# A weight stream in 12 whole units through four places, in place of 21 halves through seven

## The chip, the core and the metric

The kernel runs on one core of a Trainium2 chip. Its engines are TensorE (PE, with weight loads PEld), VectorE (DVE), ScalarE (ACT), GpSimd (POOL) and SyncE (SP), which here only issues DMAs; SP, ACT and POOL each have a DMA queue, and all queues share 16 DMA engines. SBUF has 128 partitions, and a tile "of 4 KB" holds 4 KB in each. The metric is the device time of one execution in microseconds (us), lower is better; several runs are taken and their median is compared.

## What is computed

Two attention blocks over the same 2048 x 640 input are mixed by a gate. Block A walks through 64 segments of 32 rows one after the other: the 8 memory rows that a segment puts out are the first 8 rows of the next segment's input, so the segments can't overlap freely.

```
x = A_x
g = sigmoid((x * gate_w).sum(-1, keepdims=True))
a = A(x, mem0, Wq, Wk, Wv, Wo)     # 32 heads of 192, Dm = 640
b = B(x, wqkv, wo)                 # sliding, dilated local attention
return g * a + (1 - g) * b

# A, for each of 64 segments:
h = concatenate([mem, xs], axis=1)            # 8 + 32 rows
q, k, v = h @ Wq, h @ Wk, h @ Wv              # 640 x 6144 each
p = softmax(mask(q @ k^T * scale))
o = (p @ v) @ Wo                              # 6144 x 640
mem = o[:, :8]; outs.append(o[:, 8:])
```

## The kernel before

**Order of the whole.** Block B runs first (`part_b`), then a prepass for A (`prepass`), which computes q, k and v of the segments' last rows for all segments at once, then the loop over segments (`part_a`), then the output projection of the rows that the prepass covers (`part_z`). The loop body is `segment("rest", ...)` of one segment followed by `segment("head", ...)` of the next.

**Weights.** The weights of A are cut into slices of 128 partitions, named by matrix and place. (q, p, kc) and (k, p, kc), with p = 0 to 2 and kc = 0 to 4, and (v, t, kc) have 4 KB a partition; (oa, i), i = 0 to 11, and (ob, i), i = 0 to 7, are the output weights with 3 KB a partition. A slice can be cut into two halves (a name with one more number, `_is_half`, `_parts`). Each segment reads every slice once, in the order of the code: q(0,0), k(0,0), q(1,0), q(0,1), q(0,2), k(0,1), k(0,2), q and k (0,3) and (0,4), the rest of q(1,*), k(1,*), q(2,*), k(2,*), then v(0,*), v(1,*), v(2,*), then oa and ob. A q, k or v slice is read by one burst of four matmuls of 512 columns, one for each group of 32 PE columns (`m_qk` L818, `m_v` L916); an output slice by `o_group` (L980). Between them stand the small matmuls of attention: `scores` (L870), `e_sum` (L894), `pv_half` (L941, L947), and `pick` (L997), which makes the next segment's memory rows.

**Resident and streamed.** Not all weights fit in SBUF. Most slices are loaded once and stay (`res_tiles`: wres early, wlate later). Those in `STREAM` are loaded anew in each segment, in the order of `STREAM`, into a ring of places (`slots`, tiles wst): unit n goes to place n modulo `SLOTS`. Before the change these are 21 halves (15 of 2 KB, 6 of 1.5 KB) and seven places of 2 KB. `pump` issues on SP's queue every next unit whose place is free; `release`, called behind the matmuls that read a slice, frees its place and pumps (L562 is the issue). Because SP runs in order, unit n + 1 is not issued ahead of unit n.

**Stages of the loop.** The loop body is split into four stages (`stage`, L1133 for the loop's own waits). `held()` makes SP wait, at that point of its program, for the DMAs that it issued one stage earlier, and holds back further units until the next `stage()`. No engine enters a stage before all have finished the stage two before it. The boundaries are: before `scores(1)`; behind oa 0 to 3; in the head behind q(1,0); and the loop's end. The program order of SP in one iteration is so: units freed by q(2,*), k(2,*) and the first v slices; held; units freed by later v slices; the load of the next segment's aP from zpk_dram (L752); held; units freed by oa and ob; held; in the head, units freed by the last ob and by q(0,*), k(0,*), k(1,*).

**Other transfers in a segment.** POOL's queue loads aVz (96 KB, L756), aK from in_xh_dram and from selx_dram, and stores oz_dram twice (48 KB each, L759); ACT's queue loads aG and stores out_dram (30 KB each).

**Other uses of the places.** In part B and the prepass the same tiles serve as staging for columns of Wq and Wk (`get_columns`, L599) and of v (`v_columns`, `get_slice`, L585) that are not resident. One end of place 1 also holds `st4`, the copy of a q product between ACT (L829) and DVE (L837).

**The end.** In the last segment SP issues the loads of oz (`load_oz`, L1155, four tiles at a time into resident slices no longer needed), ACT and DVE sort them (`sort_oz`), and `part_z` multiplies them (L1192), adds to a tile `b4` of B's rows (L1196) and stores. The `b4` tiles are resident half slices.

Of the kernel before, what the change touches and what calls it, by code (L numbers as in the profile page):

```python
# [11 lines left out]
F32 = mybir.dt.float32  # L12
I32 = mybir.dt.int32

SLOTS = 7
N_EARLY = 15
N_EARLY2 = 12
N_LAST = 7
LATE0 = 71680
STREAM = [("q", 0, 1, 1), ("k", 0, 1, 1), ("k", 0, 3, 1), ("q", 1, 1, 0), ("k", 1, 0, 0), ("k", 1, 3, 1), ("q", 2, 2,  # L20
          0), ("k", 2, 0, 1), ("k", 2, 1, 1), ("k", 2, 4, 1), ("v", 0, 3, 1), ("v", 1, 1, 0), ("v", 1, 4, 1), ("v", 2,
          0, 1), ("v", 2, 3, 0), ("oa", 3, 1), ("oa", 4, 1), ("ob", 2, 0), ("oa", 7, 0), ("oa", 11, 0), ("ob", 6, 0)]

STEP_PE = 3.4

# [7 lines left out]
def _width(key):  # L33
    n = 1536 if key[0] in ("oa", "ob") else 2048
    return n // 2 if _is_half(key) else n

def _parts(key):
    halves = [key + (h,) for h in range(2)]
    return halves if any(k in STREAM for k in halves) else [key]

# [53 lines left out]
class _K:  # L94
# [398 lines left out]
    def v_columns(self, t, kc):  # L493

        out = []
        for k in _parts(("v", t, kc)):
            sl = self.get_slice(k)
            out += [sl[:, f:f + 512] for f in range(0, _width(k), 512)]
        return out
# [11 lines left out]
    def weights_setup(self):  # L511
        nc, tc = self.nc, self.tc
        rest = [k for u in _slice_keys() for k in _parts(u) if k not in STREAM]
        first = ["q", "k", "v", "oa", "ob"]
        rest = sorted(rest, key=lambda k: first.index(k[0]))
        self.early, self.early2, late = rest[:N_EARLY], rest[N_EARLY:N_EARLY + N_EARLY2], rest[N_EARLY + N_EARLY2:]
        self.late = ([], [], late[-N_LAST:])
        used = 0
        for k in late[:-N_LAST]:
            used += 2 * _width(k)  # L520
            self.late[int(used > LATE0)].append(k)
        self.wres = self.ctx.enter_context(tc.tile_pool(name="wres", bufs=1))
        self.res_tiles = {}
        at = _places()[0]
        self.packed = {k: self.laid["slices"][n:n + 128 * _width(k)].rearrange("(p f) -> p f", p=128) for k, n in at.items()}
        self.wscr = self.packed
        self.wstream = self.ctx.enter_context(tc.tile_pool(name="wstream", bufs=1))
        self.slots = [self.wstream.tile([128, 1024], BF, name=f"wst{i}") for i in range(SLOTS)]
        self.slot_at, self.streaming, self.pending = 0, False, []

    def load(self, key, t):
# [42 lines left out]
    def get_slice(self, key):  # L574
        if key in self.res_tiles:
            return self.res_tiles[key]
        n = _width(key)
        if self.streaming:
            assert STREAM[self.used] == key and self.used < self.sent
            t = self.slots[self.used % SLOTS][:, 0:n]  # L580
            self.used += 1
            return self.view(t, key)
        t = self.slots[self.slot_at % SLOTS][:, 0:n]
        self.slot_at += 1
        self.nc.gpsimd.dma_start(t, self.wscr[key])  # L585
        return self.view(t, key)

    def get_columns(self, m, h):

        W = {"q": self.Wq, "k": self.Wk}[m].rearrange("(c p) f -> p c f", p=128)  # L590
        p, x = h // 2, h % 2
        out = {}
        for kc in range(self.KC):
            if (m, p, kc) in self.res_tiles:
                t = self.res_tiles[m, p, kc][:, 1024 * x:1024 * x + 1024]
            else:
                t = self.slots[self.slot_at % SLOTS]
                self.slot_at += 1
                (self.nc.sync if m == "q" else self.nc.gpsimd).dma_start(t[:], W[:, kc, 1024 * h:1024 * h + 1024])  # L599
            out[kc] = [t[:, f:f + 128] for f in range(0, 1024, 128)]  # L600
        return out

# [97 lines left out]
    def part_a(self):  # L700
# [4 lines left out]
        with ctx:  # L705
# [28 lines left out]
                        return x[:, f:f + 32]  # L734

            st = [Px[2], Px[1], KW[:, 512:1024], Px[2]]
            st4 = self.slots[1][:, 768:1024], Px[0][:, 0:256]
            st5 = (P[1][:, 1:5, 0:8, :].rearrange("p b c i -> p b (c i)"), Px[0][:, 256:512])

            psm = ctx.enter_context(tc.tile_pool(name="psm", bufs=1, space=bass.MemoryType.PSUM))  # L740
# [44 lines left out]
            def segment(part, prev, s, nxt, looped=False):  # L785
# [278 lines left out]
                if nxt is None:  # L1064
                    self.oz, self.oz_keys = {}, {}
                    self.oz_free = [k for p in range(3) for m in "qk" for k in self.res_tiles if k[:2] == (m, p) and len(k) == 3]
                    self.oz_free += [k for k in self.res_tiles if k[0] == "v" and len(k) == 3]
                    self.b4_free = [k for k in self.res_tiles if k[0] in "vqk" and len(k) == 4]
                    self.load_oz(0)
                if nxt is not None:  # L1070
                    load_seg(nxt)
# [97 lines left out]
    def part_z(self, psm, wo, tail):  # L1169

        nc = self.nc
        oz = self.oz
        kept = self.kept.values()
        for i, k in enumerate(k for k in STREAM if k in wo and k not in kept):
            t = self.res_tiles[self.b4_free[4 + i]][:, 0:_width(k)]
            nc.sync.dma_start(t, self.wscr[k])
            wo[k] = self.view(t, k)
        for n in range(1, 4):
            if n > 1:
                self.load_oz(n)  # L1180
            self.sort_oz(n)
        for n in range(4):
            b4 = self.res_tiles[self.b4_free[n]][:, 0:640]
            rows = lambda ap: ap.rearrange("(n s t) f -> n s t f", n=4, t=32)[n, :, 24:32, :]
            nc.scalar.dma_start(b4.bitcast(I32).rearrange("p (j f) -> p j f", j=4),
                                self.bsc_dram.rearrange("(n s t) j f -> n s t j f", n=4, t=32)[n, :, 24:32, :, 0:80])
            for part, f0, nf in (("oa", 0, 384), ("ob", 384, 256)):
                ps = psm[int(part == "ob")]
                for c in range(48):
                    R, j, t = c // 12, c // 3 % 4, c % 3  # L1190
                    for q in range(4):
                        nc.tensor.matmul(ps[32 * q:32 * q + 32, 0:nf],  # L1192
                                         lhsT=oz[n, q][:, 24 * (1 - R // 2) + 6 * j + 3 * (R % 2) + t, :],
                                         rhs=self.o_weights(wo, part, c), start=(c == 0), stop=(c == 47),
                                         tile_position=(0, 32 * q), skip_group_check=True)
                nc.vector.scalar_tensor_tensor(out=b4[:, f0:f0 + nf], in0=ps[:, 0:nf], scalar=self.gZ[:, n:n + 1],  # L1196
                                               in1=b4[:, f0:f0 + nf], op0=ALU.mult, op1=ALU.add)
            nc.sync.dma_start(rows(self.out2d), b4)
            if n == 0:
                tail()  # L1200
# [63 lines left out]
```

## Time and profile before

| | us |
|---|---|
| Median of 3 runs | 1554.49 (1550.25 to 1554.56) |
| The profiled execution: its own time | 1550.84 |
| its span | 1548.8 |

| Stretch, us from the start | What runs | PE busy | DMA share | GB/s |
|---|---|---|---|---|
| 0 to 180 | part B | 145.9 of 180 | 0.76 | 205 |
| 180 to 294 | prepass q, k | 112.0 of 114 | 0.81 | 235 |
| 294 to 344 | prepass v | 49.5 of 50 | 0.84 | 236 |
| 344 to 400 | first segments | 43.4 of 56 | 0.89 | 290 |
| 400 to 1400 | the loop | 195 to 197 of each 200 | 0.96 to 0.97 | 321 to 326 |
| 1484 to 1502 | loads of oz, sorting | 11.7 of 18 | 0.82 | 188 |
| 1502 to 1548 | output projection | 42.1 of 46 | 0.12 | 29 |

The DMA share is the mean share of time in which the 16 DMA engines had a packet in hand; the granted TensorE clock is 1.00 in all of the loop's stretches. An engine's busy time is the union of its instructions, so PE counts as busy also where only one of four column groups works. In names such as `wst<-in_slices_dram` the target stands left; "SPq" is SP's instruction queue, which issues DMAs and waits.

### The profile page before, as it was taken

The numbers are of one execution on the slowest core, as the hardware profiler recorded it, in microseconds if no ns is written. First come the engines' busy times: TensorE is split into PE (matmuls) and PEld (weight loads), VectorE is DVE, ScalarE is ACT, GpSimd is POOL, SyncE is SP. The second block draws the span as 40 slices with busy tenths as digits, with TensorE's granted clock in tenths as the row PEclk, the third lists the DMA queues.
The fourth block names the chain that finished last, engine by engine and source line by source line (L and its number), as shares of the span: only waits on it lengthen the run. The fifth ranks groups of instructions, "written<-read, shape, count | busy, mean of one in ns | idle before, by whom it ended". The sixth has DMA issues, their size and how long they took to land. (4 is left out here: it accounts for less than half of the span.)

```text
span 1548.8 us, 91126 instructions
## 1 busy us (share of the span) xinstructions
PE 1459.2 (94%) x36746; PEld 821.3 (53%) x36746; DVE 815.6 (53%) x2256; ACT 642.7 (41%) x1673; POOL 205.9 (13%) x432
## 2 busy tenths in 40 slices
PE   5988899997999999999999999999999999999978
PEld 3444444443555555555555555555555555555557
DVE  1787533333555555555555555555555555555510
ACT  1587532222443444344443444444444444344430
POOL 0000200200111111111111111111111111111100
PEclk9999999998999999999999999999999999999989
DMA  6778896788999999999999999999999999999970
GB/s 174 199 194 229 275 310 167 178 264 284 303 318 321 333 322 316 316 329 322 325 323 330 327 326 317 321 337 324 327 322 326 324 324 321 328 322 329 314 192 16
DMA packets 365435, 446.30 MB, mean 288 GB/s; under 512 B 123864, under 2 KB 227848, under 8 KB 365368
## 3 DMA queue, kind: packets, MB, share of 16 engines
q1 hardware_dynamic: 271080, 395.47, 77.7%
q10 hardware_dynamic: 80736, 25.44, 6.9%
q0 software_dynamic: 13552, 24.47, 4.9%
q8 instruction: 46, 0.75, 0.2%
q14 instruction: 21, 0.17, 0.0%
HBM read 407.04 MB, written 38.20 MB: 287 GB/s over the span
## 5 line engine op out<-in xcount | busy, mean ns | idle before, releaser
L825 ACT CAST aP<-psx 128x512 bf16<-128x512 f32 x128 | 68.7, 589 | 358.2 <-PE psx L818 358.2
L980 PEld LDWEIGHTS <-aP 128*32 128x32 bf16 x6144 | 162.7, 96 | 63.9 <-ACT aP L959 20.3
L916 PE MATMUL psm<-wlate_v,aHa 128*32 128x512 bf16 x2048 | 189.6, 381 | 1.1 <-issue 1.1
L818 PEld LDWEIGHTS <-aHa 128*32 128x32 bf16 x4608 | 120.1, 96 | 119.1 <-issue 20.6
L980 PE MATMUL psm<-wlate_oa,aP 128*32 128x384 bf16 x2560 | 167.7, 329 | 0.0
L840 DVE STREAM_TRANSPOSE aK<-aP 128x512 bf16<-128x512 bf16 (+1 forms) x256 | 135.0, 546 | 7.6 <-ACT aP L825 0.8
L980 PE MATMUL psm<-wst,aP 128*32 128x384 bf16 (+1 forms) x896 | 121.4, 306 | 7.4 <-DMA wst<-in_slices_dram 7.4
L980 PE MATMUL psm<-wlate_ob,aP 128*32 128x256 bf16 x2688 | 125.8, 274 | 1.0 <-issue 1.0
L818 PE MATMUL psm<-wres_q,aHa 128*32 128x512 bf16 x1280 | 119.2, 382 | 7.4 <-PEq L1133 5.2
L959 DVE CAST aP<-psx 128x128 bf16<-128x128 f32 (+2 forms) x192 | 75.6, 422 | 80.2 <-PE psx L947 80.1
L837 DVE STREAM_TRANSPOSE aP<-aP 128x512 bf16<-128x512 bf16 (+1 forms) x128 | 74.1, 579 | 79.1 <-ACT aP L825 79.1
L916 PE MATMUL psm<-wlate_v,aHb 128*32 128x512 bf16 x1152 | 115.2, 379 | 0.0
L818 PEld LDWEIGHTS <-aHb 128*32 128x32 bf16 x3072 | 77.3, 96 | 60.5 <-issue 3.0
L818 PE MATMUL psx<-wres_k,aHa 128*32 128x512 bf16 x896 | 108.1, 381 | 0.0
L925 ACT CAST aP<-psm 128x256 bf16<-128x256 f32 (+1 forms) x192 | 85.9, 447 | 47.7 <-PE psS L870 46.3
L959 ACT CAST aP<-psS 128x384 bf16<-128x384 f32 (+2 forms) x192 | 65.3, 374 | 72.5 <-PE psx L947 48.3
L756 POOL DMA_DIRECT2D aVz<-zv_dram x64 | 34.3, 535 | 443.2 <-DMA wst<-in_slices_dram 397.1
L818 PE MATMUL psx<-wst,aHa 128*32 128x512 bf16 x512 | 88.5, 382 | 2.1 <-DMA wst<-in_slices_dram 2.1
L818 PE MATMUL psm<-wres_q,aHb 128*32 128x512 bf16 x1024 | 80.4, 381 | 0.0
L916 PEld LDWEIGHTS <-aHa 128*32 128x32 bf16 x2304 | 54.7, 97 | 46.4 <-issue 16.4
L749 POOL DMA_DIRECT2D aK<-in_xh_dram x63 | 34.4, 546 | 329.0 <-PE psm L916 289.1
L941 PEld LDWEIGHTS <-aP 32*128 32x128 bf16 (+1 forms) x4096 | 43.4, 97 | 64.5 <-DVE aK L907 32.8
(181 smaller groups left out, 3222.3 us busy)
## 6 DMA issues: line engine op xcount, KB each, us to landing
wst<-in_slices_dram SPq DMA_DIRECT2D x960, 256.0 KB, 4.7
wst<-in_slices_dram SPq DMA_DIRECT2D x384, 192.0 KB, 3.8
zpk_dram<-ZS ACTq DMA_DIRECT2D x6, 2048.0 KB
aP<-zpk_dram SPq DMA_DIRECT2D x64, 192.0 KB, 3.9
wres_q<-in_slices_dram SPq DMA_DIRECT2D x12, 512.0 KB
aVz<-zv_dram POOLq DMA_DIRECT2D x64, 96.0 KB, 4.4
wlate_v<-in_slices_dram SPq DMA_DIRECT2D x10, 512.0 KB
wst<-in_A_Wk_dram POOLq DMA_DIRECT2D x14, 256.0 KB, 5.9
```

The costliest lines, as they stand in the source:

```text
L749: nc.gpsimd.dma_start(xh, row(self.xh_dram, s))
L756: nc.gpsimd.dma_start(vz[:], self.zv_dram[bass.ds(8 * s, 8)].rearrange("i r f -> r i f"))
L818: burst([nc.tensor.matmul(pq[32 * j:32 * j + 32, :], lhsT=hT[kc], rhs=sl[j], start=(kc == 0), stop=(kc == KC - 1), tile_position=(0, 32 * ...
L825: nc.scalar.copy(st[i], pqs[i])
L837: nc.vector.transpose(P[p][:, 1:5, c0:c1, :].rearrange("p b c i -> p c b i"), x)
L840: nc.vector.transpose(KT[:, c0:c1, :].rearrange("p c k -> p (c k)"), x)
L916: burst([nc.tensor.matmul(pvs[t][32 * j:32 * j + 32, :], lhsT=hT[kc], rhs=sl[j], start=(kc == 0), stop=(kc == KC - 1), tile_position=(0, 3 ...
L925: (nc.vector.tensor_copy if t == 0 else nc.scalar.copy)(Px[t][:, cs], pvs[t][:, cs])
L941: ms.append(nc.tensor.matmul(out[:, r, t, :], lhsT=v_block(2 * h + r, t)[ks, f0 - 128 * t:f1 - 128 * t], rhs=E[ks, par, EA.start + 40 * r: ...
L959: (nc.scalar.copy, nc.vector.tensor_copy)[g](x.rearrange("p (j c q) -> p j c q", j=2, q=32), pairs[g][:, :, 0:240].rearrange("p j (c q) -> ...
L980: ms.append(nc.tensor.matmul(pso[part][32 * jj:32 * jj + 32, 0:n], lhsT=oT_slot(R // 2, j, 3 * (R % 2) + t), rhs=self.o_weights(osl, part, ...
```

## The change

Twelve units are streamed in place of 21: nine whole slices (six of 4 KB, three of 3 KB) and three halves of 2 KB. There are four places: wst0 of 2 KB and wst1 to wst3 of 4 KB. Twelve is a multiple of four, so each unit always meets the same place: the three halves place 0; k(0,1), q(2,3), oa 0 place 1; k(0,2), v(0,0), oa 3 place 2; k(1,0), v(1,2), ob 4 place 3. The counts of resident tiles are set so that the same bytes are loaded at each of the earlier points. For the prepass the four tiles are seen as seven pieces of 2 KB (`pieces`, `get_piece`); a streamed v slice is staged there in two pieces. In the prepass there are four columns pieces of Wq and eight of Wk, where there were six and fourteen. Resident whole slices are put ahead of resident halves in the order of loading. `st4` moves with the wider place. The `b4` tiles at the end are the last four resident v slices, and a loop in `part_z` that reloads units that are no longer in their places becomes an assertion.

```diff
--- before.py
+++ after.py
@@ -12,14 +12,13 @@
 F32 = mybir.dt.float32
 I32 = mybir.dt.int32
 
-SLOTS = 7
-N_EARLY = 15
-N_EARLY2 = 12
-N_LAST = 7
+SLOTS = 4
+N_EARLY = 14
+N_EARLY2 = 9
+N_LAST = 6
 LATE0 = 71680
-STREAM = [("q", 0, 1, 1), ("k", 0, 1, 1), ("k", 0, 3, 1), ("q", 1, 1, 0), ("k", 1, 0, 0), ("k", 1, 3, 1), ("q", 2, 2,
-          0), ("k", 2, 0, 1), ("k", 2, 1, 1), ("k", 2, 4, 1), ("v", 0, 3, 1), ("v", 1, 1, 0), ("v", 1, 4, 1), ("v", 2,
-          0, 1), ("v", 2, 3, 0), ("oa", 3, 1), ("oa", 4, 1), ("ob", 2, 0), ("oa", 7, 0), ("oa", 11, 0), ("ob", 6, 0)]
+STREAM = [("q", 0, 0, 1), ("k", 0, 1), ("k", 0, 2), ("k", 1, 0), ("k", 1, 2, 0), ("q", 2, 3), ("v", 0, 0), ("v", 1, 2),
+          ("v", 2, 0, 0), ("oa", 0), ("oa", 3), ("ob", 4)]
 
 STEP_PE = 3.4
 
@@ -494,6 +493,11 @@
 
         out = []
         for k in _parts(("v", t, kc)):
+            if k in STREAM and not self.streaming and not _is_half(k):
+                for f in (0, 1024):
+                    sl = self.get_piece(self.wscr[k][:, f:f + 1024], self.nc.gpsimd)
+                    out += [sl[:, 0:512], sl[:, 512:1024]]
+                continue
             sl = self.get_slice(k)
             out += [sl[:, f:f + 512] for f in range(0, _width(k), 512)]
         return out
@@ -512,7 +516,7 @@
         nc, tc = self.nc, self.tc
         rest = [k for u in _slice_keys() for k in _parts(u) if k not in STREAM]
         first = ["q", "k", "v", "oa", "ob"]
-        rest = sorted(rest, key=lambda k: first.index(k[0]))
+        rest = sorted(rest, key=lambda k: (first.index(k[0]), _is_half(k)))
         self.early, self.early2, late = rest[:N_EARLY], rest[N_EARLY:N_EARLY + N_EARLY2], rest[N_EARLY + N_EARLY2:]
         self.late = ([], [], late[-N_LAST:])
         used = 0
@@ -525,7 +529,8 @@
         self.packed = {k: self.laid["slices"][n:n + 128 * _width(k)].rearrange("(p f) -> p f", p=128) for k, n in at.items()}
         self.wscr = self.packed
         self.wstream = self.ctx.enter_context(tc.tile_pool(name="wstream", bufs=1))
-        self.slots = [self.wstream.tile([128, 1024], BF, name=f"wst{i}") for i in range(SLOTS)]
+        self.slots = [self.wstream.tile([128, 2048 if i else 1024], BF, name=f"wst{i}") for i in range(SLOTS)]
+        self.pieces = [t[:, x:x + 1024] for i, t in enumerate(self.slots) for x in range(0, 2048 if i else 1024, 1024)]
         self.slot_at, self.streaming, self.pending = 0, False, []
 
     def load(self, key, t):
@@ -580,10 +585,14 @@
             t = self.slots[self.used % SLOTS][:, 0:n]
             self.used += 1
             return self.view(t, key)
-        t = self.slots[self.slot_at % SLOTS][:, 0:n]
+        return self.get_piece(self.wscr[key], self.nc.gpsimd)
+
+    def get_piece(self, src, queue):
+
+        t = self.pieces[self.slot_at % len(self.pieces)]
         self.slot_at += 1
-        self.nc.gpsimd.dma_start(t, self.wscr[key])
-        return self.view(t, key)
+        queue.dma_start(t, src)
+        return t
 
     def get_columns(self, m, h):
 
@@ -594,9 +603,7 @@
             if (m, p, kc) in self.res_tiles:
                 t = self.res_tiles[m, p, kc][:, 1024 * x:1024 * x + 1024]
             else:
-                t = self.slots[self.slot_at % SLOTS]
-                self.slot_at += 1
-                (self.nc.sync if m == "q" else self.nc.gpsimd).dma_start(t[:], W[:, kc, 1024 * h:1024 * h + 1024])
+                t = self.get_piece(W[:, kc, 1024 * h:1024 * h + 1024], self.nc.sync if m == "q" else self.nc.gpsimd)
             out[kc] = [t[:, f:f + 128] for f in range(0, 1024, 128)]
         return out
 
@@ -734,7 +741,7 @@
                         return x[:, f:f + 32]
 
             st = [Px[2], Px[1], KW[:, 512:1024], Px[2]]
-            st4 = self.slots[1][:, 768:1024], Px[0][:, 0:256]
+            st4 = self.slots[1][:, 1536:1792], Px[0][:, 0:256]
             st5 = (P[1][:, 1:5, 0:8, :].rearrange("p b c i -> p b (c i)"), Px[0][:, 256:512])
 
             psm = ctx.enter_context(tc.tile_pool(name="psm", bufs=1, space=bass.MemoryType.PSUM))
@@ -1065,7 +1072,7 @@
                     self.oz, self.oz_keys = {}, {}
                     self.oz_free = [k for p in range(3) for m in "qk" for k in self.res_tiles if k[:2] == (m, p) and len(k) == 3]
                     self.oz_free += [k for k in self.res_tiles if k[0] == "v" and len(k) == 3]
-                    self.b4_free = [k for k in self.res_tiles if k[0] in "vqk" and len(k) == 4]
+                    self.b4_free = [self.oz_free.pop() for _ in range(4)]
                     self.load_oz(0)
                 if nxt is not None:
                     load_seg(nxt)
@@ -1171,10 +1178,7 @@
         nc = self.nc
         oz = self.oz
         kept = self.kept.values()
-        for i, k in enumerate(k for k in STREAM if k in wo and k not in kept):
-            t = self.res_tiles[self.b4_free[4 + i]][:, 0:_width(k)]
-            nc.sync.dma_start(t, self.wscr[k])
-            wo[k] = self.view(t, k)
+        assert all(k in kept for k in STREAM if k in wo)
         for n in range(1, 4):
             if n > 1:
                 self.load_oz(n)
```

## The prediction

> **What bounds the kernel now.** I read the page's utilisation and slices first, then the windows, the groups by tile, the DMA rows, PE's waits, and last the timeline of single segments.
>
> ```profile
> span 1548.8 us, 91126 instructions
> PE 1459.2 (94%) x36746; PEld 821.3 (53%) x36746; DVE 815.6 (53%) x2256; ACT 642.7 (41%) x1673; POOL 205.9 (13%) x432
> ...
> 1000.00:1200.00 200.00, 195.44 (x5883) 112.72 (x5878) 114.87 (x350) 85.56 (x254) 31.62 (x59) 1.00 0.97 326
> ...
> wst<-in_slices_dram SPq DMA_DIRECT2D x960, 256.0 KB, 4.7
> wst<-in_slices_dram SPq DMA_DIRECT2D x384, 192.0 KB, 3.8
> ...
> PE psm L916 <- DMA wst<-in_slices_dram: 4.9, 15, 0.7
> ```
>
> In the settled loop (the windows row: PE, PEld, DVE, ACT, POOL, granted clock, DMA share, GB/s) two things are full at once: PE 195 of 200 us at a granted clock of 1.00, and the DMA engines 0.97 of the time. PE's waits put only 4.9 us on the stream. That is too little, and two timelines of the same place, v slice (2,0), show why:
>
> ```profile
> 1016.06 0.39 PE L916 MATMUL psm<-wlate_v,aHa 128*32 128x512 bf16 x2
> 1016.07 0.39 PE L916 MATMUL psm<-wst,aHa 128*32 128x512 bf16 x2
> ...
> 1188.32 0.39 PE L916 MATMUL psm<-wlate_v,aHa 128*32 128x512 bf16 x2
> 1188.97 0.39 PE L916 MATMUL psm<-wst,aHa 128*32 128x512 bf16 x2 [0.26 <-DMA wst<-in_slices_dram]
> ```
>
> Half of this slice is resident, half streamed. In the first segment all four matmuls start together. In the second the two streamed ones start 0.65 us after the resident two, and the page books 0.26 as idle, because the resident pair still runs. So I measured stalls by the length of a segment instead (start of slice q(0,0) to the next start). Over segments 3 to 60 the mean is **17.41 us**, the shortest, reached by several, is **16.94**, the longest 18.7. The gap of 0.47 us is what the stream costs: in 72% of the segments the half of v (2,0) is first read within 0.06 us of its landing, in 33% that of k (0,1), in 30% that of k (2,1). By the median, 256 KB needs 4.7 us from issue to landing, while the shortest landing in the trace (192 KB) is 2.4 us. The difference is queue: between landings of neighbouring units in the quiet middle of a segment lie 0.66 us, which is 8 packets an engine at the 84 ns median of a 2048-byte packet. The loop is bound by PE at 16.94 and by the DMA queue just above that.
>
> **The change, part by part.** Bytes stay: 15 x 2 KB + 6 x 1.5 KB = 39 KB a partition before, 3 x 2 + 6 x 4 + 3 x 3 = 39 KB after; room stays too, 7 x 2 = 3 x 4 + 2 = 14 KB.
>
> *DMA work.* The packet records of the trace have medians of 65, 84, 121 and 159 ns for 1536, 2048, 3072 and 4096 bytes (the last two from loads of resident slices and the prepass), and 9 ns for the semaphore packet. An engine moves 8 partitions. Before: 15 x (8 x 84 + 9) + 6 x (8 x 65 + 9) = 13.39 us a segment. After: 3 x 681 + 6 x (8 x 159 + 9) + 3 x (8 x 121 + 9) = 12.66. That is 0.73 us less, 4%, in a queue that is full. It lies beside PE and can give back at most the 0.47.
>
> *SP.* 9 issues fewer at 328 ns, 3.0 us a segment. SP mostly waits for PE to free a place, so I count 0.
>
> *Places.* A place is now refilled when a whole slice has been read, and used when a whole one has landed. This is the part that can cost, so I followed each place through one segment at 16.94 us. Times are from the start of q(0,0); reads are from the timeline near 1005 us, a read holds its place 0.4 us, and the issue comes 0.1 later (trace: 0.1 to 0.2). A transfer that finds the queue empty lands 1.9 us + its packets after issue (shortest landing 2.4 less 0.53 of packets); else one service (0.68, 0.98 or 1.28 us) after the one ahead.
>
> - k(0,1): freed by oa 0, issued 13.0, lands 16.2, needed 18.1.
> - k(0,2): freed by oa 3, issued 13.5, lands 1.28 behind, 17.5, needed 18.3. Spare 0.8.
> - k(1,0): freed by ob 4, issued 16.5, lands 19.7 to 20.0, needed 20.8. Spare 0.7.
> - half of k(1,2): issued 17.4, lands 20.7, needed 21.2. Spare 0.5.
> - q(2,3): freed by k(0,1), issued 18.6, lands 22.0, needed 22.5. Spare 0.5.
> - v(0,0), v(1,2), half of v(2,0), oa 0, oa 3, ob 4 and the half of q(0,0): spare 1.4 or more.
>
> Against that spare stand the small transfers of POOL's and ACT's queues. Their price shows in the steps between landings: units 0, 1 and 2 of the old order take 1.82 + 0.90 + 1.24 us on average where their packets and the 192 KB of aP take 3 x 0.68 + 0.65, so 1.27 us goes to them. The old victim was v(2,0), whose step is 1.50 for 0.68, since aVz is issued beside it at 5.6; in the new order aVz falls beside the half of v(2,0) and oa 0, with 1.4 us and more to spare. The new victim is k(0,2): with none of the 1.27 in its way it has 0.8 spare, with all of it it is 0.47 late. I take half, since the last and dearest of these (oz_dram, issued at 16.0) showed its delay 1.5 to 3 us after its issue, when k(0,2) is through. That leaves 0.15 us spare with a scatter of some 0.45 (one step's middle 80% spans 0.7 to 0.8), a mean loss of about 0.12, and 0.03 for the next three. So **residual stall 0.15 us a segment**, bounds 0 (all spare holds) and 0.7 (k(0,2) fully late and the gate below too).
>
> ```profile
> SPq L1133 <- DMA wst<-in_slices_dram: 61.5, 127, 1.1
> ```
>
> *The loop's stages.* The row is SP's own wait inside the loop, 61.5 us in 127 waits: at each held() it waits until the transfers of the stage before have landed, and no engine passes the next boundary until it has. The last transfer that the boundary before scores(1) asks for was the half of v(1,4), landing at 8.6; it becomes the half of v(2,0), at 8.3 to 9.1. PE passes at 10.0, so nothing is charged; cover 0.9 us. Behind SP's wait stand ob 4's issue (free only at 9.8) and aP's, neither moved later.
>
> *Outside the loop.* The prepass loads 12 pieces of columns instead of 20; PE is busy 112 of 114 us there, so 0 (it could give back 1.4 us, its wait for in_A_Wk_dram). The first two segments take 25.5 and 23.0 us while the DMA queue is full: 4% of the stream's share, about -1 us. At the end SP is the chain:
>
> ```profile
> by line: SPq L1155 62.4%; DMA wlate_v<-oz_dram 12.5%; DMA wres_q<-bsc_dram 8.4%; issue 5.9%; PE psm L916 5.8%; DVE wres_q L1196 1.7%; SPq L562 1.4%; PE psm L1192 1.3%; PE psS L870 0.8%; PE psS L894 0.3%; ACTq L1164 0.1%; ACT wres_q L1164 0.
> ```
>
> Ahead of its first load of oz three stream transfers become one, freed by v(1,2) and not v(1,4): about -1 us. The four b4 tiles move from halves to whole v slices, read long before: 0.
>
> **Sum.** 60 settled segments x (0.47 - 0.15) = -19, and -2 outside: -21 us. The profiled execution would go from a span of 1548.8 to 1528, in its own time 1550.8 to 1530; against the median of the runs shown, 1554.5, that is **1533 us**.
>
> The Trainium skill, "DMA: Bandwidth & Descriptors", section Anatomy of one DMA, fits a DMA (of the other issue path) as 2.0 us + bytes / 436 GB/s. An estimate by it is 2.6 us for 256 KB and 3.2 for 512 KB, so every place above would be in time and the sum would be -30. The trace disagrees for this queue: 4.7 us for 256 KB, so I keep the rows.
>
> **Rivals.**
> *Slower: two whole slices in a row.* k(0,1) and k(0,2) sit side by side and are freed 0.5 us apart. If the queue keeps its old depth, a landing is unit 2's 4.77 us plus the 0.60 of the bigger unit, 5.37, against 4.8 from issue to need: 0.57 late each segment, and with q(2,3) late by 0.15, 0.72 instead of 0.47: 60 x 0.25 = +15, **1570 us**. It decides from the point where k(0,2) lands more than 5.3 us after its issue, that is over 0.47 late. For it: the landings under load. Against it: the old depth was seven units, now at most three stand ahead.
> *No change: the stall moves.* All of the 1.27 us falls on k(0,2), 0.47 late: **1553**. For it: mean steps have that size; against it: where the oz_dram delay showed.
> *Bytes and not packets bind.* Then 0.73 us is not saved, the queue still asks 17.4 us a segment and, with k(0,2) late in a part of the segments by up to 0.13 on average, it ends at 1554 to 1562. Against it: quiet steps of 0.66 us are 262 KB at 397 GB/s, above the loop's mean of 326.
> The Trainium skill, same page, section Where 436 GB/s comes from, names about 358 GB/s as the HBM limit of a core, by which this rival would hold. The trace's 397 in the quiet steps disagrees.
> *All spare holds:* 16.94 a segment, -30: **1524**.
>
> **How the numbers follow.** A difference of 0.3% (4.7 us) is about what can be told from none here. Forecast with 0 to 0.3 us of residual stall (1524 to 1542, the rival with all spare inside it) 0.60; two whole slices in a row 0.25; the stall moves 0.10; bytes bind 0.05, of it 0.03 slower. So faster 0.60, same 0.12, slower 0.28. The range reaches from a floor of 1519 (the -30, with 5 of scatter between medians) to the slower rival's 1570; the forecast's own is 1520 to 1542.
>
> **What would show it.** Right: segments at 16.94 to 17.2, v(2,0) read at once, 512 KB landing in 3.2 to 4.8 us, DMA share below 0.95. Wrong: k(0,2) (L818, psx<-wst) starting late after k(0,1), scores(1) (L870) waiting at a boundary, or 4096-byte packets well above 159 ns.

## The result and the profile after

The changed kernel takes **1660.07 us** (median of 4 runs, 1653.09 to 1662.03) against 1553.28 for the kernel before on the same chip: a ratio of 1.0697, 95% interval 1.067 to 1.0724. It is slower by 107 us, far outside the range, in the direction that the forecast gave 0.28.

First the page's line of the span and its line of busy time by engine:

```profile
span 1658.8 us, 89256 instructions
PE 1483.2 (89%) x36746; PEld 823.0 (50%) x36746; DVE 815.7 (49%) x2254; ACT 642.2 (39%) x1673; POOL 203.3 (12%) x426
```

Two rows of the view by stretches (PE, PEld, DVE, ACT, POOL, granted clock, DMA share, GB/s):

```profile
600.00:800.00 200.00, 183.69 (x5452) 103.53 (x5444) 105.89 (x324) 78.55 (x234) 29.26 (x54) 1.00 0.90 300
1000.00:1200.00 200.00, 181.05 (x5292) 101.64 (x5294) 102.08 (x307) 77.75 (x230) 28.71 (x53) 0.97 0.88 287
```

PE is busy 181 to 184 of 200 us where it was 195. The granted clock is 1.00 in the first of the two rows as before and 0.97 in the second, and PE is no busier there, so the lost time is idle time. The DMA engines went from 0.97 to 0.88 and 0.90 busy: nothing is full any more. What was lost must lie in waits of one for the other, and the single segments show them.

The segments say how much. From q(0,0) to the next q(0,0), over segments 3 to 60, the mean is **19.28 us** (17.41 before), the shortest 17.37 (16.94). From its first segment to its last the loop takes 1225.4 us against 1110.5, which is +114.9; all the rest of the span takes 433.4 against 438.3, which is -4.9. The loss lies wholly in the loop.

The rows of the stream in the view of DMA issues (KB each, median us from issue to landing):

```profile
wst<-in_slices_dram SPq DMA_DIRECT2D x384, 512.0 KB, 5.8
wst<-in_slices_dram SPq DMA_DIRECT2D x192, 384.0 KB, 4.3
wst<-in_slices_dram SPq DMA_DIRECT2D x192, 256.0 KB, 3.6
```

PE's waits for the stream (us in total, times, longest): first, of the kernel before, at the q and k slices that go to psx, between 420 and 1460 us; then, of the changed kernel, at the like slices and at the v slices, between 420 and 1560 us:

```profile
PE psx L818 <- DMA wst<-in_slices_dram: 0.9, 3, 0.4
...
PE psx L825 <- DMA wst<-in_slices_dram: 67.0, 79, 1.7
PE psm L923 <- DMA wst<-in_slices_dram: 15.9, 36, 0.9
```

SP's waits at the loop's stages:

```profile
SPq L1140 <- DMA aP<-zpk_dram: 120.2, 61, 3.0
SPq L1140 <- DMA wst<-in_slices_dram: 97.6, 66, 2.4
```

A 512 KB unit lands 5.8 us after its issue by the median, where the working had 3.2 to 4.0. PE now waits 67 us for k slices in 79 waits, where the like row had 0.9 in 3. SP's wait for the stream at the stages rose from 61.5 us in 127 waits to 97.6 in 66, and its 120.2 us for aP are new. These waits of SP delay no issue that PE then misses: of all units only ob 4 goes out more than 0.3 us after its place is free (0.6 on average), and it still lands 2.25 us before its read. The timeline of PE in one segment, only the reads of streamed units, shows both places (start, duration, idle time before and what ended it):

```profile
1008.19 0.39 PE L825 MATMUL psx<-wst,aHa 128*32 128x512 bf16 x4
1009.61 0.40 PE L825 MATMUL psx<-wst,aHa 128*32 128x512 bf16 x4 [1.03 <-DMA wst<-in_slices_dram]
...
1016.06 0.39 PE L923 MATMUL psm<-wst,aHa 128*32 128x512 bf16 x4
1018.48 0.40 PE L923 MATMUL psm<-wst,aHa 128*32 128x512 bf16 x4 [0.63 <-DMA wst<-in_slices_dram]
```

k(0,1) is read at 1008.19. The read of k(0,2) should follow 0.2 us later, as reads do here that wait for nothing; it comes 1.42 us later, and PE stands idle for 1.03 of them. The second gap is v(1,2), which the place table had with 1.4 us to spare.

The next table sets each unit of the working beside what the trace has: the mean over segments 5 to 60 from issue to landing. The trace has 16 signals for each transfer, one for each DMA engine, and the read of k(0,2), late in every segment, starts 0.04 us after the 16th. "First" is the earliest engine, "last" the latest. "PE stalls" is the mean time by which the read (for the gate: `scores(1)`) follows the work ahead of it later than it does when nothing is late.

| Unit | worked out | first of 16 | last of 16 | PE stalls |
|---|---|---|---|---|
| k(0,1) | 3.2 | 3.28 | 5.26 | 0.34 |
| k(0,2) | 4.0 | 4.22 | 6.21 | 1.0 (late in every segment) |
| k(1,0) | 3.2 to 3.5 | 3.27 | 5.0 | 0.05 |
| half of k(1,2) | 3.3 | 3.18 | 4.8 | 0 |
| q(2,3) | 3.4 | 3.23 | 4.67 | 0 |
| v(1,2) | spare 1.4 or more | 3.03 | 5.22 | 0.40 |
| half of v(2,0), gate of scores(1) | cover 0.9 | 3.29 | 5.43 | 0.28 |

The column of the first engine agrees with the times worked out, within some 0.2 us. The last engine comes 1.4 to 2.2 us after it. The stalls sum to 2.07 of the 2.34 us (19.28 - 16.94) that a segment now loses; the rest is scattered.

The stalls don't fade, because they form a ring. From the read of k(0,2) PE needs 2.5 us to the read of k(1,0), whose place v(1,2) takes 0.4 later; that lands 5.2 later; from its read PE needs 4.0 to oa 3, whose place k(0,2) takes 0.5 later; and that lands after 6.2: 2.5 + 0.4 + 5.2 + 4.0 + 0.5 + 6.2 = 18.8 us, within 0.5 of the segment. (In some segments v(1,2) lands before PE comes to it; there the ring isn't tight.) Two landings stand in the ring, and where it is tight each microsecond that they grow is a microsecond of the segment. In the kernel before the like ring (half v(2,0), oa 3, half k(0,1), q(2,2)) has landings of 4.3 and 4.7 and closes at about 17.0.

### The profile page after: what moved, and what is told of

Its sections match the earlier page's. It is cut to its first block, busy times and chain, and to the rows that moved or that the text cites. A ratio compares the mean times of both kernels' runs of the same rounds, so it can differ in the third digit from the quotient of the medians.

```text
span 1658.8 us, 89256 instructions
## 1 busy us (share of the span) xinstructions
PE 1483.2 (89%) x36746; PEld 823.0 (50%) x36746; DVE 815.7 (49%) x2254; ACT 642.2 (39%) x1673; POOL 203.3 (12%) x426
## 5 line engine op out<-in xcount | busy, mean ns | idle before, releaser
L825 PEld LDWEIGHTS <-aHa 128*32 128x32 bf16 x4608 | 123.5, 97 | 207.7 <-issue 111.1
L987 PEld LDWEIGHTS <-aP 128*32 128x32 bf16 x6144 | 166.9, 96 | 52.2 <-ACT aP L966 13.6
L923 PE MATMUL psm<-wlate_v,aHa 128*32 128x512 bf16 x1664 | 148.7, 380 | 1.6 <-issue 1.4
L987 PE MATMUL psm<-wlate_oa,aP 128*32 128x384 bf16 x2560 | 147.4, 329 | 0.0
L825 PE MATMUL psx<-wst,aHa 128*32 128x512 bf16 x640 | 76.4, 390 | 69.3 <-DMA wst<-in_slices_dram 68.9
L825 PEld LDWEIGHTS <-aHb 128*32 128x32 bf16 x3072 | 72.4, 98 | 69.1 <-issue 10.2
L886 DVE TENSOR_TENSOR aK<-aK,aSel 128x224 bf16<-128x224 bf16 x128 | 35.2, 275 | 122.9 <-ACT aK L885 122.9
L923 PE MATMUL psm<-wst,aHa 128*32 128x512 bf16 x640 | 75.6, 384 | 17.4 <-DMA wst<-in_slices_dram 16.7
L923 PEld LDWEIGHTS <-aHa 128*32 128x32 bf16 x2304 | 56.6, 96 | 63.8 <-issue 34.0
L877 PEld LDWEIGHTS <-aK 128*32 128x32 bf16 (+1 forms) x4096 | 45.9, 91 | 67.1 <-issue 32.5
L825 PE MATMUL psx<-wres_k,aHa 128*32 128x512 bf16 x1024 | 78.7, 383 | 0.0
```

The source lines that it names most:

```text
L825: burst([nc.tensor.matmul(pq[32 * j:32 * j + 32, :], lhsT=hT[kc], rhs=sl[j], start=(kc == 0), stop=(kc == KC - 1), tile_position=(0, 32 * ...
L877: ms.append(nc.tensor.matmul(out, lhsT=k, rhs=q, start=(half == 0 and R2 == 0), stop=(half == 1 and R2 == 2), tile_position=(ks.start, 32 ...
L886: nc.vector.tensor_tensor(out=E, in0=E, in1=self.mask[h].unsqueeze(1).to_broadcast([128, 2, 112]), op=ALU.mult)
L923: burst([nc.tensor.matmul(pvs[t][32 * j:32 * j + 32, :], lhsT=hT[kc], rhs=sl[j], start=(kc == 0), stop=(kc == KC - 1), tile_position=(0, 3 ...
L987: ms.append(nc.tensor.matmul(pso[part][32 * jj:32 * jj + 32, 0:n], lhsT=oT_slot(R // 2, j, 3 * (R % 2) + t), rhs=self.o_weights(osl, part, ...
```

## The experiments

Three things changed together: the order of use (which slices are streamed), places of 4 KB, and transfers of 512 KB. The first runs try to take them apart.

**E1, one slice moved.** k(0,4) is streamed in place of k(0,2).

```diff
-STREAM = [("q", 0, 0, 1), ("k", 0, 1), ("k", 0, 2), ("k", 1, 0), ...
+STREAM = [("q", 0, 0, 1), ("k", 0, 1), ("k", 0, 4), ("k", 1, 0), ...
```

> The changed kernel with one unit moved: k(0,4) is streamed and k(0,2) is resident, so the two whole slices that were read 0.2 us apart are read 1.6 us apart. A segment of the changed kernel takes 19.28 us, of it 1.0 us is k(0,2) waiting for its landing in every segment. Order theory (a place's time from freeing to need is shorter than a loaded landing, at this pair first): that 1.0 us goes, some 0.2 comes back at v(0,0), whose place is freed 1.4 us later: 18.5 us a segment, about 1612 us. Rival, the stall moves: the queue is what is late, the wait shows up at k(1,0) or q(2,3) instead, 1650 to 1660 us.

1652.14 us, ratio 1.0683 (1.0642 to 1.0724), segment 18.96: the time that the rival gave, not the 1612 of the order theory. k(0,4) lands after 6.23 us as k(0,2) did, and now in time; but k(1,0) is late in 89% of the segments, the half of k(1,2) in 96%, and v(1,2) stalls PE by 0.63. PE's timeline in this run, v(0,0) and then v(1,2):

```profile
1024.85 0.40 PE L923 MATMUL psm<-wst,aHa 128*32 128x512 bf16 x4 [0.28 <-DMA wst<-in_slices_dram]
1027.41 0.40 PE L923 MATMUL psm<-wst,aHa 128*32 128x512 bf16 x4 [0.77 <-DMA wst<-in_slices_dram]
```

In this segment both whole v slices are caught at their landing (v(0,0) in about half of all segments, v(1,2) in nine of ten). To give one unit more time doesn't shorten the ring as long as its neighbours have none.

**E2, the transfers undone.** Same order, same places; each whole unit is moved by two DMAs of half its width, one behind the other.

```diff
-            self.nc.sync.dma_start(self.slots[n][:, 0:_width(k)], self.wscr[k])
+            for f in range(0, _width(k), _width(k) if _is_half(k) else _width(k) // 2):
+                g = f + (_width(k) if _is_half(k) else _width(k) // 2)
+                self.nc.sync.dma_start(self.slots[n][:, f:g], self.wscr[k][:, f:g])
```

> The changed kernel with the same places and the same order, but each whole unit is sent for as two transfers of half its width, issued one behind the other: packets of 2048 and 1536 bytes in place of 4096 and 3072, and 21 issues a segment again. Size theory (the long landing is that of the big transfer: 5.2 us from issue, where the slowest of the 16 engines ends 2 us after the first, and 4096-byte packets that take 194 ns on average for a median of 159): landings of a whole unit fall by 0.5 us or more, time falls to 1600 us or below. Order theory: nothing changes but 0.7 us more packet work in a queue that is no longer full, 1655 to 1670 us.

1644.14 us, 1.063 (1.0591 to 1.067), segment 18.89, between the two theories. The difference to the changed kernel is 16 us by the medians (1660.07 - 1644.14), which come from separate sets of runs, and 10 by the ratios to the kernel before (0.7%). It is a net price: the pair k(0,1), k(0,2) now takes four issues, and the last goes out 0.98 us after its place is free, where the whole k(0,2) went out 0.04 after. v(1,2) no longer stalls PE, but k(0,2) does by 1.17 and k(0,1) by 0.32: from the first issue of this pair to its last landing there are still 6.7 us.

**E3, places and transfers undone, the new order kept.** The kernel before with its seven places of 2 KB, streaming the slices of the new order as adjacent halves.

```diff
-STREAM = [("q", 0, 1, 1), ("k", 0, 1, 1), ("k", 0, 3, 1), ...
+STREAM = [("q", 0, 0, 1), ("k", 0, 1, 0), ("k", 0, 1, 1), ("k", 0, 2, 0), ("k", 0, 2, 1), ...
```

> The kernel before, with its seven places of 2 KB and 21 halves, but the halves are those of the changed kernel's slices, both halves of a slice one behind the other: the order of the change without its large places and transfers. Order theory (the loss is that k(0,1) and k(0,2), k(1,0), v(1,2) are needed too soon after their room is freed, whatever the pieces): about as slow as the changed kernel with split transfers, 18.5 to 19.0 us a segment, 1630 to 1660 us. Place theory (the loss is that 4 KB must be read before any of it is refilled): below 1600 us.

1618.65 us, 1.0452 (1.041 to 1.0494), segment 18.54. This is between the theories too. Against the kernel before, the new slices as adjacent halves cost 68 us (1618.65 - 1550.24), the places another 25 (E2 less E3), the transfers 16; by the ratios it is 70, 28 and 10. That the 68 are the price of the order alone isn't shown: the halves of a slice now also stand one behind the other, and E15 comes back to this. k(0,2) still stalls PE, by 1.15; k(0,1) and v(1,2) don't. SP's part shows here: it issues the four halves of k(0,1) and k(0,2) at 0.4 to 0.5 us each, so the last goes out 0.98 us after its place is free.

**E5, an even order through the new places.** The slices are chosen so that the reads lie as far apart as they did before.

```diff
-STREAM = [("q", 0, 0, 1), ("k", 0, 1), ("k", 0, 2), ("k", 1, 0), ("k", 1, 2, 0), ("q", 2, 3), ("v", 0, 0), ("v", 1, 2),
-          ("v", 2, 0, 0), ("oa", 0), ("oa", 3), ("ob", 4)]
+STREAM = [("k", 0, 0, 1), ("q", 0, 2), ("k", 0, 4), ("k", 1, 1), ("q", 2, 4, 0), ("k", 2, 2), ("v", 1, 0), ("v", 1, 4),
+          ("v", 2, 0, 0), ("oa", 0), ("oa", 4), ("oa", 8)]
```

> Twelve units of the same sizes through the same four places, but other slices, chosen so that every place has 4.25 to 6.2 us from its freeing to the next need and no two whole ones are read within 1 us: half k(0,0), q(0,2), k(0,4), k(1,1), half q(2,4), k(2,2), v(1,0), v(1,4), half v(2,0), oa 0, oa 4, oa 8. Order theory: the stalls at k(0,1), k(0,2) and v(1,2), 1.75 us a segment in the changed kernel, mostly go: 17.2 to 17.7 us a segment, 1540 to 1570 us, level with the kernel before. Size theory: any order of whole units waits for landings of 5 us and more: above 1610 us.

1560.46 us, 1.007 (1.0042 to 1.0098), segment 17.66. The same places, the same 512 KB, the same bytes, and 100 of the 107 us are gone. Its stretch and its row of 512 KB:

```profile
800.00:1000.00 200.00, 189.83 (x5654) 106.64 (x5648) 110.70 (x336) 81.99 (x242) 30.03 (x56) 1.00 0.92 316
...
wst<-in_slices_dram SPq DMA_DIRECT2D x384, 512.0 KB, 5.3
```

Landings are only 0.5 us shorter than in the changed kernel. Two things are different: the whole q and k slices of the head are issued 1.5 us apart and not 0.5, so their landings don't stack up on one read, and by its plan no place has less than 4.25 us from its freeing to the next need, where the changed kernel's working had 3.9 at the least. What each of the two is worth wasn't taken apart. k(0,4) is still caught at its landing in 75% of the segments, v(1,4) in 58%, the half of v(2,0) in 89%, by 0.2 us each on average.

**E15, the even order through small places.** If the three prices add up, this one should beat all.

```diff
+STREAM = [("k", 0, 0, 1), ("q", 0, 2, 0), ("q", 0, 2, 1), ("k", 0, 4, 0), ("k", 0, 4, 1), ("k", 1, 1, 0), ("k", 1, 1, 1),
...
```

> The slices of the even order (the kernel before's rhythm with whole slices, 1560.46 us through places of 4 KB) as 21 adjacent halves through the seven places of 2 KB. If the costs found so far add up (order alone +68, places of 4 KB +25, transfers of 512 KB +16 us), this order through small places is 41 us below the 1560: 1515 to 1525. If the even order had already taken the cost of places and transfers away, because no unit waits for its place there, it comes out at 1550 to 1560, no better than the kernel before.

1618.52 us, 1.0424 (1.0382 to 1.0467), segment 18.53: neither theory, and 58 us slower than the same order in whole units. The prices don't add up: as adjacent halves through small places the even order is no faster than the uneven one (E3, 1618.65 us). So there the adjacent halves cost 66 to 70 us by the ratios whatever the order, and the order's own price is shown only through the large places, by E5. SP's waits between 800 and 1000 us in this run and then the wait of the q and k slices for the stream (420 to 1500 us):

```profile
SPq L1133 <- DMA wst<-in_slices_dram: 21.5, 11, 2.9
```
```profile
PE psx L818 <- DMA wst<-in_slices_dram: 41.3, 56, 1.7
```

Once a segment SP stands 2.0 us (21.5 / 11) at a stage. Behind that wait are queued five issues (both halves of oa 4 and of oa 8, the half of k(0,0)) at 0.4 to 0.5 us each and aP's, and behind them q(0,2): its halves go out 1.04 and 1.42 us after their places are free, where in E5, with three issues in that spot, the whole slice goes out 0.04 us after, though SP waits longer at its stages there (32.2 us between 800 and 1000 us). q(0,2) then stalls PE. That reading is from the trace and wasn't tried by itself.

**E6, E7 and E13, the small transfers.** The forecast saw the danger to k(0,2) in the small transfers of the other queues. E6 leaves out of the loop one oz_dram store and the load of aG, E7 the load of aVz, E13 all of them, so that only the stream and aP are left.

```diff
+                    if not looped:
+                        load_vz(s)
...
+                if not looped:
+                    store_z(s, 0)
...
+                    if not looped:
+                        load_a4(s)
```

> The changed kernel; in the loop it leaves out one of the two stores of oz_dram (that of aK) and the load of aG, two small transfers of POOL's and ACT's queues that are issued 0.9 and 1.4 us behind k(0,1) and land with k(0,2). A copy of 3 MB at the very start fills oz_dram, so the total is to be read by the length of a segment. Interference theory: k(0,2) lands 6.2 us after issue because the slowest of the 16 engines carries these between its packets; without them it lands near 5, its stall of 1.0 us falls below 0.4, a segment takes 18.3 to 18.7 us instead of 19.3, some -35 to -60 us. Rival, two transfers of 512 KB in a row are slow by themselves: 19.1 to 19.3 us a segment, total within 15 us of the changed kernel.

> The changed kernel without the load of aVz in the loop (POOL's 96 KB; the values used are stale). It lands with v(1,2), whose transfer takes 5.2 us and 0.4 us of PE's time. Chain theory: the length of a segment is a closed chain, k(0,2) read, 2.5 us of PE, k(1,0) read and its place freed, v(1,2) lands 5.2 us after issue, 4.0 us of PE, oa 3 read and its place freed, k(0,2) lands 6.2 us after issue: 18.8 us with the issue steps. Shortening the one landing by 0.7 us or more shortens the segment by as much until the next chain: 18.5 to 18.8 us, 1610 to 1632 us. Rival, the wait at v(1,2) is slack that k(0,2) would take up anyway: 1645 to 1660 us.

> The changed kernel with every transfer but the stream and aP left out of the loop: the loads of aVz, xh, selx and aG, both stores to oz_dram and the store of out are gone there (oz_dram and out are filled once ahead of everything, so the result and the total time are not comparable; read the segment, start of q(0,0) to the next, which is 19.28 us in the changed kernel). Theory 'the slices of 4 KB one behind another are late by themselves': k(0,2) still lands 5.8 us or more after its issue, is late in 90% of the segments by 0.7 us or more, and the segment is 18.5 or more. Rival 'the small transfers beside them stretch the landings': k(0,2) lands in 5.2 us or less, its stall falls below 0.3 us, and the segment is 17.2 or less.

| | k(0,2) lands | late | v(1,2) lands | segment |
|---|---|---|---|---|
| changed kernel | 6.24 | 100% | 5.20 | 19.28 |
| E6 | 6.03 | 100% | 4.95 | 18.76 |
| E7 | 6.21 | 100% | 5.03 | 19.08 |
| E13 | 5.70 | 96% | 4.60 | 18.27 |

(These means take in one segment more than the table of the units.) In full time, E6 took 1644.68 us (1.061, 1.0576 to 1.0645) and E7 1642.94 (1.0597, 1.0544 to 1.065); E13's total holds a large copy ahead of the loop and says nothing. E6 and E7 miss what their theories said, by too small an effect: E6 was to bring the landing of k(0,2) near 5 us, E7 that of v(1,2) down by 0.7. In E7 it went down by 0.17 us and the segment by 0.20, which is what the ring asks for, but small. E13's rival wanted k(0,2) in 5.2 us or less and a segment of 17.2; the theory wanted 5.8 and 18.5 or more. It lies between, nearer the theory: of the 2.34 us that a segment loses the small transfers make 1.0, and the stream all by itself 1.33. E13's stretch (POOL has nothing left to do) and its timeline at the old spot:

```profile
800.00:1000.00 200.00, 185.58 (x5480) 105.77 (x5468) 107.38 (x326) 80.70 (x238) 0.00 (x0) 0.99 0.87 288
```
```profile
1027.40 0.39 PE L828 MATMUL psx<-wst,aHa 128*32 128x512 bf16 x4
1028.60 0.40 PE L828 MATMUL psx<-wst,aHa 128*32 128x512 bf16 x4 [0.81 <-DMA wst<-in_slices_dram]
```

With 0.13 of the DMA engines' time free and no other queue than SP's, PE still stands idle for 0.81 us before k(0,2) in this segment (0.49 on average; 0.83 in the changed kernel). Its first engine is done after 4.04 us, its last after 5.70.

**E9, E12, E16 and E17, the kernel before and its own ring.** The other side of the same theory: if a ring of landings sets the segment, the kernel before gains where its late reads are moved back. E9 streams half of v(2,2) in place of v(2,0), E12 half of v(2,1), E16 half of k(0,2), k(2,2) and v(2,1) in place of k(0,1), k(2,1) and v(2,0), E17 besides this q(1,2) for q(1,1).

```diff
-STREAM = [("q", 0, 1, 1), ("k", 0, 1, 1), ... ("q", 1, 1, 0), ... ("k", 2, 1, 1), ... ("v", 2, 0, 1), ...
+STREAM = [("q", 0, 1, 1), ("k", 0, 2, 1), ... ("q", 1, 2, 0), ... ("k", 2, 2, 1), ... ("v", 2, 1, 1), ...
```

> The kernel before with one unit moved: the streamed half is one of v(2,2) and not of v(2,0), so it is needed 1.3 us later. In the kernel before, v(2,0) waits for its landing in 72% of the segments, 0.3 us on average. If the queue is nearly full but not the bound: 0.2 to 0.3 us a segment are won, 1535 to 1543 us. If the DMA queue is the bound, the stall moves to other units: 1550 to 1556 us.

> The kernel before with the streamed half of v(2,0) replaced by one of v(2,1), read 0.2 us later. With v(2,2), 1.3 us later, the place came free so late that SP issued the next half of ob 6 behind aP and the stall moved to q(0,1) and k(0,1). By 0.2 us that order is kept: up to 0.15 us a segment won, 1540 to 1548 us. If the ring passes every delay on: 1549 to 1556 us.

> The kernel before with three of its halves a slice later in the order of use: k(0,2), k(2,2) and v(2,1) streamed by half in place of k(0,1), k(2,1) and v(2,0). Theory 'the segment is set by the closed chain of place, landing and read': the two reads that were caught at their landing have a slice (0.4 us) more each, and the segment goes from 17.41 to 17.1 or below, the time to 1532 to 1546. Rival 'the queue of the stream is full, 17.4 us of work a segment': landings move by as much as the reads do, and the time stays within 4 us of 1550, as it did with v(2,1) alone (1549.12).

> The kernel with the shorter chain (1545.5 us, ratio 0.9947 to the kernel before, segment 17.19) with one more streamed half a slice later: q(1,2) in place of q(1,1), the unit that was still read at its landing in 37% of its segments. Theory 'closed chain of place, landing and read': the read has 0.4 us more, v(0,3) behind it in the same place has 0.79 us to spare and gives up 0.4, the segment falls to 17.0 to 17.1 and the time to 1534 to 1541. Rival 'the queue is full': the next unit takes the place as the late one, segment and time stay at 17.19 and within 3 us of 1545.

| | us | ratio to the kernel before | segment of the profiled execution |
|---|---|---|---|
| E9 | 1560.35 | 1.0076 (1.0047 to 1.0105) | 17.59 |
| E12 | 1549.12 | 0.9986 (0.9968 to 1.0004) | 17.34 |
| E16 | 1545.50 | 0.9947 (0.9922 to 0.9973) | 17.19 |
| E17 | 1546.87 | 0.9977 (0.9958 to 0.9997) | 17.34 |

E9 misses by its own side effect: v(2,2) is read later, so its place goes to the half of ob 6 later, SP issues aP first, and k(0,1) is late in 84% of the segments. E12 changes nothing clear of the noise: v(2,1) is caught in 58% of the segments where v(2,0) was in 72%, but k(0,1) in 49% and no longer 33%. **E16 is faster than both kernels**, by 0.5% than the kernel before; its time lies at the end of the range that the ring gave, its segment just above it. The profiled execution (1537.46 us) is the fastest of its 12 runs, so 17.19 flatters it. E17 was to gain by the same theory and misses: it does what it says for q(1,2), late in 12% and not 37%, and gains nothing: v(2,1) goes from 35 to 42%, k(1,0) from 4 to 23%. E16's stretch shows how little room is left:

```profile
800.00:1000.00 200.00, 196.01 (x5945) 114.66 (x5940) 114.60 (x352) 86.06 (x255) 31.93 (x59) 1.00 0.97 326
```

PE 196 of 200 us, the DMA engines 0.97. In the kernel before, lateness taken from one unit mostly goes to the next. That fits a full queue; but its own ring closes at 17.0 us, so near to 16.94 that these runs don't separate the two. In the changed kernel nothing is full, and lateness comes from the ring.

## Why the prediction was wrong, point by point

All three signs of being wrong that the prediction named came: k(0,2) starts late after k(0,1), `scores(1)` waits at its boundary, and the 4096-byte packets take 194 ns by the mean.

- **What binds before** (PE at 16.94, the queue just above it): nothing speaks against it. E12 moved a read and gained nothing, E17 no more than E16, and E16 gained 0.5% with the DMA engines still 0.97 busy.
- **DMA work, 13.39 to 12.66 us a segment.** The medians were right: 159, 121 and 84 ns for 4096, 3072 and 2048 bytes in the loop. The sum was not, for it was made of medians. The means after are 194, 149 and 89 ns (before: 94 for 2048 and 75 for 1536 bytes), since some 3% of the 4096-byte packets take 600 ns or more. Over a segment an engine's packets cost 2.47 us above their medians, 1.67 before: 12.66 + 2.47 = 15.1 against 13.39 + 1.67 = 15.1. The saving of 0.73 us was 0.
- **SP, 9 issues fewer, 0:** held for the changed kernel, where the issue of the k pair follows its place by 0.04 us. E3 and E15 show what the fewer issues are worth where several places come free at once: up to 1.4 us of lateness.
- **Places: the step that failed.** "A transfer that finds the queue empty lands 1.9 us + its packets after issue" turned out to be the time of the first engine. It was taken from the shortest landing of the trace. The reader waits for the last of 16, 1.4 to 2.2 us later in the new order. The trace of before had it: half of ob 2, which waits 1.1 us for SP and so goes into the emptiest queue, lands after 3.2 us by the mean (first engine 2.07), where the formula gives 1.9 + 0.53 = 2.4; half of q(0,1) lands after 3.8 (first 2.45) where it gives 2.6. With the 1.4 to 2.2 us on each row of the place table, k(0,2) with its 0.8 us of spare, k(0,1) with 1.9 and v(1,2) with 1.4 would all have been at or past their limits.
- **Half of the 1.27 us of small transfers on k(0,2):** a price of the wrong thing. Those beside it (E6) move its landing by 0.2 us; all of them together by 0.5 (E13). Alone it is still late.
- **Residual stall 0.15 us, at most 0.7:** it is 2.34. The upper bound was made of one late unit and the gate; the ring wasn't seen, since the table followed each place once through a segment that still took 16.94 us. With the late landings put in, the table doesn't close on itself until the segment is 18.8.
- **The gate before scores(1), cover 0.9:** gone. The half of v(2,0) was to land 0.9 to 1.7 us ahead of PE; it lands at 11.8 us of the new segment, 0.6 before `scores(1)` starts at 12.4, and scores(1) is held 0.28 us on average. The cover of before was misread as well: in the quiet segments the half of v(1,4) lands at 9.0 to 9.5 us, not at 8.6.
- **Outside the settled loop, -2:** the first two segments were to give 1 us and cost 1 (49.5 us together, 48.5 before); everything outside the loop gave 4.9 where 1 was forecast.
- **The rival "two whole slices in a row"** named the place and the point from which it decides (5.3 us from issue to landing; 6.21 came). Its mechanism, a queue that keeps its old depth, isn't what the trace shows: the DMA engines are 0.88 to 0.90 busy, and what is late is the last of the 16. It was priced at +15 us, as one late unit less the stall that goes away; with k(0,1), v(1,2) and the gate behind it in one ring it was +107. "The stall moves" was right for E1, but not as a case of no change. "Bytes bind" is refuted: GB/s fell to 285 to 300 in the loop, and E5 moves the same bytes at 316.
- The figure of the Trainium skill ("DMA: Bandwidth & Descriptors", Anatomy of one DMA), which gave an estimate of 3.2 us for 512 KB, is met here by the first of the 16 engines of k(0,1) (3.28 us), and the landing, 5.8 us by the median, is far from it.

What stays open: why a few single 4096-byte packets take four times their median, also with no other queue at work (in E13, 3% at 565 ns or more), and what makes the spread of the 16 so different from unit to unit. It is shown that it happens and what it costs, not where it comes from. That these packets are what makes the last engine late is argued from the two figures and not tried by itself.

## What to carry to other kernels

Before places are made larger and fewer, draw the ring: read, place freed, issue, landing, next read, until it comes back to the first read; the sum of its steps is a lower bound of the loop's period, and each landing in it has to be a typical one (to the last of the 16 engines), not the shortest. Which slices are streamed mattered more here than how: with the same bytes, places and transfers the order was worth 100 us, and transfers of half the size 10 to 16. But prices found one at a time need not add up: cut into adjacent halves and put through small places, the good order lost 58 of the 100 us again. And a ring that is in time in the mean at the old period is no proof; put a microsecond of lateness on a unit and see whether anything takes it off again.

## What the runs showed of the hardware

One DMA's 16 engines don't finish together. For k(0,2) the first is done 4.22 us after issue, the middle one at 4.92, the last at 6.21; for the 256 KB units of the kernel before the last comes some 0.7 us after the middle one (0.6 to 1.1). In the changed kernel the step from the middle to the last is largest, 1.2 to 1.7 us, for three pairs of neighbours issued 0.5 to 0.9 us apart: k(0,1) and k(0,2), k(1,0) and the half of k(1,2), v(1,2) and the half of v(2,0). Closeness alone doesn't make it: in E5 oa 4 and oa 8 go out 0.45 us apart and have 0.4 us, and only k(0,4) has more than 1.0. Packets of 4096 bytes have the same median, 159 ns, in the changed kernel and in E5, so the slow ones among them are few (3% at 600 ns or more in the changed kernel, 2.2% in E5).

Without any of the small transfers of the other queues (E13), the mean of a 4096-byte packet went from 194 to 192 ns, the landing of k(0,2) from 6.2 to 5.7 us, and the step from the middle to the last engine became 0.9 to 1.1 us for those six units. The segment became 1.0 us shorter.
